# Two chunks of every sequence per block of 512 tokens, units going sequence by sequence, and weight steps set closer together

## The chip, the cores and the metric

The kernel runs on one core of a Trainium2 chip. The metric is device time in microseconds (us): the median of several executions of the same program. A profile is one further execution, recorded by the hardware profiler.

## The reference

Four sequences of 768 tokens go through a retention layer (8 heads of 64) and two feed-forward layers:

```python
for t in range(S):
    state = gamma * state + einsum('bhd,bhe->bhde', k[:, :, t], v[:, :, t])
    y[:, :, t] = scale * einsum('bhd,bhde->bhe', q[:, :, t], state)
x = y.transpose(0, 2, 1, 3).reshape(3072, 512)
h = x @ w_in                                # 512 -> 2048
x = where(h > 0, h, exp(min(h, 0)) - 1) @ w_out
h = x @ w_in2                               # 512 -> 1024
s = h * softmax(h)
out = (s - mean(s)) / sqrt(var(s) + 1e-6) * g_ln @ w_out2
```

All tensors are fp32. `gamma` differs by head and is constant in time.

## The kernel before

**Units and blocks.** The retention is cut into chunks of 64 tokens. A unit is one chunk of one sequence with all 8 heads, 48 units in all, `u = 12 * sequence + chunk`. A block is 512 tokens, so 8 units, and there are 6 blocks; before the change a block is 8 chunks in that order, so a border between sequences can lie inside a block. For a unit TensorE computes the scores (`att_scores`, L191), the product of decayed keys with values that goes into the state (L195), and the values (`att_values`: L232 from the state of the chunk before, which a sequence's first chunk does not have, and L235 from the masked scores). VectorE masks the scores (L199), updates the state (L212; L210 for a first chunk) and writes the scaled output into `xf` (L240). ScalarE copies halves of the state (L215). GpSimd scales the keys (`scale_k`, L185) and makes the decayed state that the next unit adds to (L219). A unit's q, k and v are one load of 576 KB (`load_unit`, L180) into one of four buffers.

**Feed-forward 1.** Each fp32 product is three matmuls of rounded parts: high by high, high by low, low by high (`mm3`, L71 to L73). A slot `s` is one of 16 slices of the hidden width for one block: `ff1_in(s)`, 12 matmuls of 512 columns into `hp`; the ELU (`elu_a` on ScalarE, `elu_b` and `elu_c`); and `ff1_out(s - 2)`, 12 matmuls into `acc`, two slots later.

**Weights.** In block 0 the weights of feed-forward 1 come in as 64-bit words of 512 KB a slice and are turned to fp32 parts on the chip, 32 slices in the order `order1`. The parts of one slice are: `load_w` (SP); `top_w`, a cast on ScalarE and a memset of 16-bit fields on GpSimd (L117, L118); `bits_w`, two shift-and-or operations on VectorE, the second reading the first's result (L124, L125); `high_w`, a cast on ScalarE (L135); `low_w`, a subtraction on VectorE (L143). A call `prep_w(order, n)` issues parts of several slices:

```python
high_w(n - 2); top_w(n + 1); bits_w(n); low_w(n - 2); load_w(n + 3)
```

Two such calls stand in each slot of block 0, and four in the head. Slot `s` of block 0 thereby finishes slices `2s + 1` and `2s + 2`, in the kernel before as in the one after.

**The order.** Every engine runs its instructions in program order, and the program sets that order by hand (`manual_schedule`). The head (L441 to L479) goes through units 0 to 7 of block 0 with no feed-forward work beside them, because the first `ff1_in` needs all 512 tokens. In it units turn through three sets of PSUM banks; two of these later hold `acc`. Where a unit's output is written, `split_x0` makes the high part `xh` (ScalarE, L260) and the low part `xl` (L261; units 0 to 5 on GpSimd, 6 and 7 on VectorE). Then come slots: before the change unit 8 stands in slot 0 and unit `9 + s // 2` in each odd slot, so that block `b`'s units run beside the slots of block `b - 1`. After slot 15 `split_xh` and `split_xl` (L248, L253) cut the next block's tokens. In the last block of feed-forward 1 the second layer's weights are prepared by the same steps in the order `order2`. The rest of the kernel, feed-forward 2 with its normalization by 128 tokens, is not touched except for the rows to which the output goes.

Of the kernel before, what the change touches and what calls it, by code (L numbers as in the profile page):

```python
# [39 lines left out]
PRE = (2, 3, 4, 5)  # L40
AHEAD = 1
# [3 lines left out]
def tile_retention_ffn(ctx, tc, qkv, w_in1, w_out1, w_in2, w_out2, g_ln, dmask, odec, kdec, gdec, ident_in, out):  # L45
# [10 lines left out]
    gm_sb = const.tile([P, 2, 2 * D], F32, name="gm_sb")  # L56
# [5 lines left out]
    kd_sb = small.tile([P, NP], F32, name="kd_sb")  # L62
    g_sb = small.tile([P, NF2], F32, name="g_sb")
    half_n = small.tile([P, 232], F32, name="half_n")[:, :1]
# [10 lines left out]
    with tc.manual_schedule():  # L75
# [8 lines left out]
        e_p = ph1.enter_context(tc.tile_pool(name="e", bufs=3))  # L84
        g_p = ph1.enter_context(tc.tile_pool(name="g", bufs=3))
# [35 lines left out]
        def bits_w(x):  # L121
            raw = raw_t.pop(x)
            low, t = raw[:, :, 0], raw[:, :, 1]
            nc.vector.scalar_tensor_tensor(low, low, 29, top_t.pop(x), ALU.logical_shift_right, ALU.bitwise_or)  # L124
            nc.vector.scalar_tensor_tensor(t, t, 3, low, ALU.logical_shift_left, ALU.bitwise_or)  # L125
            abs_t[x] = t
# [18 lines left out]

        def prep_w(order, n):

            at = lambda i: order[i] if 0 <= i < len(order) else None
# [29 lines left out]
        def load_unit(u):  # L178
            t = at_p.tile([P, 18 * D], F32, tag="in", name="in", bufs=4)
            nc.sync.dma_start(out=t, in_=qkv[u])  # L180
            in_t[u] = t

        def scale_k(u):
            kt = in_t[u][:, KR:KR + 4 * D].rearrange("p (h d) -> p h d", h=4)
            nc.gpsimd.tensor_tensor(kt, kt, kd_sb.unsqueeze(2).to_broadcast([P, 4, D]), ALU.mult)  # L185

        def att_scores(u, banks):
# [4 lines left out]
            if u % NCH < NCH - 1:  # L192
# [9 lines left out]
        def att_state(u, v):  # L202

            c = u % NCH
            if c == NCH - 1:
                return
            st = at_p.tile([P, 2, 2 * D], F32, tag="state", name="state")
# [5 lines left out]
            s2 = at_p.tile([P, 2 * D], F32, tag="s2", name="s2")  # L213
            for j in range(2):
                nc.scalar.copy(s2[half(1 - j)], st[half(j), 1 - j])  # L215
            s_t[u + 1] = (st, s2)
            if c + 1 < NCH - 1:
                sg_t[u + 1] = at_p.tile([P, 2, 2 * D], F32, tag="sg", name="sg", bufs=1)
                nc.gpsimd.tensor_tensor(sg_t[u + 1], st, gm_sb, ALU.mult)  # L219

        def att_values(u, banks):
            c = u % NCH
# [14 lines left out]
        def att_done(u, v):  # L237
            ci = u % UPB
# [17 lines left out]
        def split_x0(ts, engine):  # L256
            if 0 not in x_t:
                x_t[0] = [x_p.tile([P, KD, TB], F32R, tag=tag, name=tag) for tag in ("xh", "xl")]
            xh, xl = x_t[0]
            nc.scalar.copy(xh[:, :, ts], xf[:, :, ts])  # L260
            engine.tensor_tensor(xl[:, :, ts], xf[:, :, ts], xh.bitcast(F32)[:, :, ts], ALU.subtract)  # L261
# [3 lines left out]
        def ff1_in(s):  # L265
# [4 lines left out]
            for cc in range(KD):  # L270
                o = cc * P
                mm3(hp, wh[:, o:o + P], wl[:, o:o + P], xh[:, cc, :], xl[:, cc, :], cc == 0, cc == KD - 1)
# [54 lines left out]
        N2 = NT // P  # L327
        yin, ysp, h2, zc_t, rs_t, zt_t, op_t, zr_t = {}, {}, {}, {}, {}, {}, {}, {}
# [97 lines left out]
        def ff2_out(i, kks=range(NF2)):  # L426
# [26 lines left out]
        scale_k(1)  # L453
        att_scores(0, sets[0][0])
        att_mask(0, sets[0][1])
        att_state(0, sets[0][1])
        load_unit(2)
        slot = -1
        for u in range(UPB):
# [7 lines left out]
            if u < 2:  # L467
                load_w(order1[u])
# [184 lines left out]
```

## Time and profile before

| | |
|---|---|
| median of 3 runs | 892.26 us (891.64 to 892.56) |
| the profiled execution | 892.1 us, span 890.3 us |
| TensorE (PE) busy | 861.9 us, 97% of the span |
| VectorE (DVE) busy | 437.4 us, 49% |
| ScalarE (ACT) busy | 327.1 us, 37% |
| GpSimd (POOL) busy | 336.4 us, 38% |
| moved by DMA | 97.94 MB, mean 110 GB/s |

Busy TensorE time counts matmuls that overlap and whose ends are modelled, so 97% does not say that the array works at its peak. PEclk is the granted clock of TensorE: 1.00 is 2.4 GHz, 0.50 is 1.2 GHz. In a timeline row the text in brackets is the idle time of that engine just before the instruction, and what ended it; "x16" means that 16 instructions of one kind are merged. The first start of an instruction that follows without a pause can lie before the recorded end of the one ahead of it, since they overlap; distances from start to start are what an instruction costs its engine.

### The profile page before, as it was taken

Reading aid. Unit: us, or ns where it says so; the run is one execution under the profiler, and the core shown is the slowest. Engines: PE = TensorE matmul, PEld = TensorE weight load, DVE = VectorE, ACT = ScalarE, POOL = GpSimd, SP = SyncE. Lnnn points to the kernel's source line nnn. Section 1 sums busy time; section 2 is a strip of 40 time slices with the busy share of each in tenths; the row PEclk is TensorE's granted clock in tenths of the full one; section 3 lists DMA queues with packets and bytes.
Section 4 is the critical chain, followed back from the end, with each engine's and each line's share of the span. In section 5 each row is a group of like instructions: output and inputs, shape, how many; then the busy total and the mean of one; then the engine's idle time right before and its main releaser. Section 6 shows DMA issues by size and latency. Waiting matters only on the chain.

```text
span 890.3 us, 15643 instructions
## 1 busy us (share of the span) xinstructions
PE 861.9 (97%) x6432; PEld 703.6 (79%) x6432; DVE 437.4 (49%) x733; ACT 327.1 (37%) x574; POOL 336.4 (38%) x323
## 2 busy tenths in 40 slices
PE   5599999999999999999999999999999999999998
PEld 4478887888888888888888878888778888888886
DVE  3489996222432234222422246786755555555542
ACT  3367774221332232222322234443343333333333
POOL 5545552322333323233323235563333333333330
PEclk9589999999999999999999999999999999999999
DMA  9457762211131112111130024230454444444432
GB/s 322 159 161 229 221 219 72 84 49 33 54 102 54 54 52 78 54 54 54 34 111 16 1 95 154 95 94 25 145 175 142 142 142 145 150 151 147 142 118 72
DMA packets 59879, 97.94 MB, mean 110 GB/s; under 512 B 4896, under 2 KB 41504, under 8 KB 59808
## 3 DMA queue, kind: packets, MB, share of 16 engines
q1 hardware_dynamic: 59808, 96.95, 33.6%
q8 instruction: 50, 0.82, 0.4%
q14 instruction: 21, 0.17, 0.1%
HBM read 72.29 MB, written 24.64 MB: 109 GB/s over the span
## 4 chain that ended last, share of the span: by engine, by line
PE 80%; DVE 12%; DMA 3%; issue 2%; POOL 1%; ACT 1%; SPq 0%; DVEq 0%; ACTq 0%; POOLq 0%
PE hp L72 13%; PE hp L73 13%; PE hp L71 12%; PE acc L71 9%; PE acc L73 8%; PE acc L72 8%; PE op L73 4%; PE op L72 4%; PE op L71 4%; DVE raw L124 2%; DVE raw L125 2%; PE ab L191 1%; DVE w1il L143 1%; DMA in<-in_qkv 1%; DVE w1ol L143 1%
## 5 line engine op out<-in xcount | busy, mean ns | idle before, releaser
L300 POOL TENSOR_TENSOR gl<-e,gh 128x512 fp32r<-128x512 f32 x80 | 108.3, 1354 | 219.2 <-issue 147.8
L71 PE MATMUL hp<-xh,w1ih 128*128 128x512 f32 x384 | 151.9, 396 | 5.1 <-ACT w1ih L135 2.6
L71 PE MATMUL acc<-gh,w1oh 128*128 128x512 f32 x384 | 153.7, 400 | 0.0
L72 PE MATMUL hp<-xl,w1ih 128*128 128x512 f32 x384 | 151.7, 395 | 0.9 <-DVE xl L253 0.9
L73 PE MATMUL hp<-xh,w1il 128*128 128x512 f32 x384 | 151.4, 394 | 0.2 <-DVE w1il L143 0.2
L73 PE MATMUL acc<-gh,w1ol 128*128 128x512 f32 x384 | 150.0, 391 | 0.0
L72 PE MATMUL acc<-gl,w1oh 128*128 128x512 f32 x384 | 149.8, 390 | 0.0
L281 ACT ACTIVATE e<-hp 128x512 f32<-128x512 f32 x80 | 47.7, 597 | 198.6 <-PE hp L73 197.2
L290 DVE TENSOR_SCALAR e<-e 128x512 f32<-128x512 f32 x80 | 36.0, 450 | 147.2 <-ACT e L281 147.2
L292 ACT CAST gh<-e 128x512 fp32r<-128x512 f32 x96 | 59.6, 621 | 97.0 <-DVE e L291 78.1
L71 PEld LDWEIGHTS hp<-xh,w1ih 128*128 128x128 f32 x384 | 73.1, 190 | 20.9 <-ACT xh L260 2.7
L199 DVE TENSOR_TENSOR pt<-ab,dm_sb 128x256 f32<-128x256 f32 x43 | 18.2, 422 | 143.3 <-PE ab L235 133.9
L72 PEld LDWEIGHTS hp<-xl,w1ih 128*128 128x128 f32 x384 | 73.2, 191 | 17.4 <-DVE xl L253 1.6
L73 PEld LDWEIGHTS hp<-xh,w1il 128*128 128x128 f32 x384 | 73.2, 191 | 16.1 <-DVE w1il L143 0.9
L71 PEld LDWEIGHTS acc<-gh,w1oh 128*128 128x128 f32 x384 | 72.1, 188 | 16.2
L73 PEld LDWEIGHTS acc<-gh,w1ol 128*128 128x128 f32 x384 | 72.1, 188 | 16.0 <-DVE w1ol L143 0.5
L72 PEld LDWEIGHTS acc<-gl,w1oh 128*128 128x128 f32 x384 | 72.1, 188 | 14.1
L370 POOL TENSOR_SCALAR z<-z,st 128x1024 f32<-128x1024 f32 x22 | 28.0, 1275 | 140.2 <-DVE st L368 140.2
L73 PE MATMUL op<-w2oh,zl 128*128 128x512 f32 (+1 forms) x192 | 74.2, 386 | 2.6 <-DVE zl L411 2.6
L118 POOL MEMSET raw<- 128x512 uint16 x48 | 60.9, 1269 | 38.4 <-ACT top L117 14.6
L219 POOL TENSOR_TENSOR sg<-state,gm_sb 128x256 f32<-128x256 f32 x40 | 36.1, 902 | 103.0 <-DVE state L212 95.0
L71 PE MATMUL op<-w2oh,zh 128*128 128x512 f32 (+1 forms) x192 | 74.3, 387 | 0.4 <-ACT zh L405 0.4
(112 smaller groups left out, 1450.1 us busy)
## 6 DMA issues: line engine op xcount, KB each, us to landing
in<-in_qkv SPq DMA_DIRECT2D x48, 576.0 KB, 4.4
raw<-in_w_in SPq DMA_DIRECT2D x24, 512.0 KB, 3.6
raw<-in_w_out SPq DMA_DIRECT2D x24, 512.0 KB, 3.6
t_dr<-t SPq DMA_DIRECT2D x22, 512.0 KB, 2.8
zt<-t_dr SPq DMA_DIRECT2D x88, 128.0 KB, 2.5
y_dr<-yt SPq DMA_DIRECT2D x24, 256.0 KB, 2.6
yin<-y_dr SPq DMA_DIRECT2D x24, 256.0 KB, 3.5
out<-ot SPq DMA_DIRECT2D x23, 256.0 KB, 2.7
```

What stands on the lines that cost most here:

```text
L71: nc.tensor.matmul(o, lh, rh, start=first, stop=False)
L72: nc.tensor.matmul(o, lh, rl, start=False, stop=False)
L73: nc.tensor.matmul(o, ll, rh, start=False, stop=last)
L118: nc.gpsimd.memset(quarter(x, 3, U16), 0)
L124: nc.vector.scalar_tensor_tensor(low, low, 29, top_t.pop(x), ALU.logical_shift_right, ALU.bitwise_or)
L199: nc.vector.tensor_tensor(pt, v[:, :, :2 * C], dm_sb, ALU.mult)
L219: nc.gpsimd.tensor_tensor(sg_t[u + 1], st, gm_sb, ALU.mult)
L281: nc.scalar.activation(e, h_t[s], AF.Exp)
L290: nc.vector.tensor_scalar(e, e, 1.0, -1.0, ALU.min, ALU.add)
L292: nc.scalar.copy(gh, e)
L300: engine.tensor_tensor(gl, e, gh.bitcast(F32), ALU.subtract)
L370: nc.gpsimd.tensor_scalar(z, z, st[:, 5:6], 1.0, ALU.add, ALU.mult)
```

## The change

**Order of units.** The input is cut so that block `b` holds chunks `2b` and `2b + 1` of each of the four sequences. Unit `u` has chunk `chunk(u)`; units `u` and `u + 4` are two chunks in a row of one sequence, so the first four units have no state, and four states are kept. `place(u)` puts the four sequences' 128 tokens side by side in `xf`; the output rows of 128 tokens are mapped back by `row(i)`.

**The head** is written anew. Per unit `u` the order is: loads from a table, `scale_k(u + 1)`, `att_decay(u + 1)` (the decayed state, now made when the later unit is near, by a broadcast table that is loaded together with the key decays), `att_state(u)`, `att_scores(u + 1)`, `att_mask(u + 1)`, `att_values(u)`, `att_kv(u + 1)` (the L195 product, now apart from the scores), then weight parts and splits from the tables `MID` and `END`. All `xl` parts go to VectorE. Units 0 to 3 and 7 load into a pool of four buffers that is closed after the head, all other units into three buffers; before there were four for all.

**Slot 0** does its products with `xh` first and the four with `xl` last. Unit 8 is processed in slot 1 (its scores still in the head), unit `8 + s // 2` in each odd slot up to 13, unit 15 in slot 14, unit 16 in slot 15 and from there as before.

**Weight steps.** `bits_w` is cut in two: `bits_w` (first operation) and `merge_w` (second). A step finishes a slice in one go.

```diff
+        def merge_w(x):
+            low, t = abs_t[x]
             nc.vector.scalar_tensor_tensor(t, t, 3, low, ALU.logical_shift_left, ALU.bitwise_or)
             abs_t[x] = t
...
         def prep_w(order, n):
-            if at(n - 2):
-                high_w(at(n - 2))
-            if at(n + 1):
-                top_w(at(n + 1))
-            if at(n):
-                bits_w(at(n))
-            if at(n - 2):
-                low_w(at(n - 2))
-            if at(n + 3):
-                load_w(at(n + 3))
+            step_w(merge_w, order, n)
+            step_w(high_w, order, n)
+            step_w(bits_w, order, n + 1)
+            step_w(low_w, order, n)
+            step_w(top_w, order, n + 2)
+            step_w(load_w, order, n + 4)
...
         def load_unit(u):
-            t = at_p.tile([P, 18 * D], F32, tag="in", name="in", bufs=4)
+            pool, n = (first_p, 4) if u < 4 or u == UPB - 1 else (at_p, 3)
+            t = pool.tile([P, 18 * D], F32, tag="in", name="in", bufs=n)
...
+        chunk = lambda u: u // UPB * (UPB // B) + u % UPB // B
+        place = lambda u: u % B * (UPB // B) + u % UPB // B
...
-            s_t[u + 1] = (st, s2)
-            if c + 1 < NCH - 1:
-                sg_t[u + 1] = at_p.tile([P, 2, 2 * D], F32, tag="sg", name="sg", bufs=1)
-                nc.gpsimd.tensor_tensor(sg_t[u + 1], st, gm_sb, ALU.mult)
+            s_t[u + B] = (st, s2)
+
+        def att_decay(u):
+            if 0 < chunk(u) < NCH - 1:
+                sg_t[u] = at_p.tile([P, 2, 2 * D], F32, tag="sg", name="sg", bufs=SG)
+                four = lambda t: t.rearrange("p a (m d) -> p (a m) d", m=2)
+                nc.gpsimd.tensor_tensor(four(sg_t[u]), four(s_t[u][0]), kg_sb[:, 1].unsqueeze(2).to_broadcast([P, 4, D]), ALU.mult)
...
+            if s == 0:
+                terms = [(w, xh, cc) for cc in range(KD) for w in (wh, wl)] + [(wh, xl, cc) for cc in range(KD)]
+                for i, (w, x, cc) in enumerate(terms):
+                    nc.tensor.matmul(hp, cut(w, cc), x[:, cc, :], start=i == 0, stop=i == len(terms) - 1)
...
+        LOADS = {0: (2, 3, "0"), 1: (4,), 2: (5,), 3: (6,), 4: (7, "1"), 5: (8,), 6: ("2", "3", 9), 7: ("4", 10)}
+        MID = {4: (w(bits_w, 0),), 5: (w(merge_w, 0),), 6: (xl(0, 1, 2, 3),)}
+        END = {
+            3: (w(top_w, 0), xh(0, 1, 2, 3)),
+            5: (w(high_w, 0), xh(4, 5)),
+            6: (xh(6),),
+            7: (xh(7), w(low_w, 0), w(top_w, 1), xl(4, 5), xl(6), xl(7), w(bits_w, 1), w(top_w, 2), w(merge_w, 1)),
+        }
         nc.gpsimd.memset(half_n, -0.5)
         new_top()
+        nc.sync.dma_start(out=kg_sb, in_=kgdec)
         load_unit(0)
         nc.sync.dma_start(out=dm_sb, in_=dmask)
-        nc.sync.dma_start(out=kd_sb, in_=kdec)
         load_unit(1)
-        nc.sync.dma_start(out=gm_sb, in_=gdec)
         nc.sync.dma_start(out=od_sb, in_=odec)
...
         for u in range(UPB):
...
+            banks, v = sets[u % 3]
+            nxt, w = sets[(u + 1) % 3] if u + 1 < UPB else both
+            for x in LOADS.get(u, ()):
+                load_unit(x) if isinstance(x, int) else step_w(load_w, order1, int(x))
+            scale_k(u + 1)
+            if u + 1 >= B:
+                att_decay(u + 1)
+            att_state(u, v)
+            att_scores(u + 1, nxt)
+            att_mask(u + 1, w)
+            att_values(u, banks)
+            att_kv(u + 1, nxt)
+            for f in MID.get(u, ()):
+                f()
+            att_done(u, v)
+            for f in END.get(u, ()):
+                f()
+        first.close()
...
+        att_state(UPB, both[1])
+        scale_k(UPB + 1)
+        att_decay(UPB + 1)
+        step_w(high_w, order1, 1)
+        step_w(bits_w, order1, 2)
+        step_w(low_w, order1, 1)
+        slot = 1
...
-            u = UPB + AHEAD + s // 2 if s % 2 else (UPB if s == 0 else NU)
+            u = UPB + s // 2 + (s > NF1 - 2) if s % 2 else (2 * UPB - 1 if s == NF1 - 2 else NU)
...
                     att_scores(u + 1, both[0])
+                    att_kv(u + 1, both[0])
...
+                if u + 2 < NU:
+                    att_decay(u + 2)
...
-                load_w(order2[0])
-                load_w(order2[1])
-                prep_w(order2, -1)
+                for i in range(-4, 0):
+                    prep_w(order2, i)
```

`step_w(f, order, i)` calls `f` for slice `i` unless that was done already. In `LOADS` a number is a unit and a string a weight slice.

## Rows read from the trace of the kernel before

**Rows 1.** The page's chain of waits that ended last, shares of the span

```profile
PE 80%; DVE 12%; DMA 3%; issue 2%; POOL 1%; ACT 1%; SPq 0%; DVEq 0%; ACTq 0%; POOLq 0%
```

**Rows 2.** Windows: busy us (x instructions) of PE, PEld, DVE, ACT, POOL; PEclk, DMA share, GB/s

```profile
20.00:25.00 5.00, 2.44 (x75) 1.81 (x70) 3.69 (x5) 2.11 (x5) 5.00 (x5) 0.50 0.99 399
...
36.10:41.90 5.80, 5.76 (x16) 3.83 (x17) 0.74 (x1) 0.00 (x0) 1.34 (x2) 0.52 0.29 119
...
100.00:110.00 10.00, 10.00 (x57) 7.98 (x59) 9.69 (x17) 7.24 (x14) 6.41 (x6) 1.00 0.69 236
```

**Rows 3.** Timeline, TensorE, head: start us, us, what [idle before <- releaser]

```profile
18.41 0.71 PE L191 MATMUL acc<-in 64*64 64x64 f32 x16 [0.92 <-DMA in<-in_qkv]
...
21.03 0.70 PE L191 MATMUL ab<-in 64*64 64x64 f32 x15
...
31.61 0.49 PE L232 MATMUL acc<-in,state 64*64 64x64 f32 x8 [2.81 <-DVE state L212]
...
36.14 0.80 PE L71 MATMUL hp<-xh,w1ih 128*128 128x512 f32 x1 [2.55 <-ACT xh L260]
```

**Rows 4.** Timeline, GpSimd and VectorE, head

```profile
20.48 2.35 POOL L261 TENSOR_TENSOR xl<-xf,xh 128x1024 fp32r<-128x1024 f32 x1
...
21.72 1.65 DVE L124 SCALAR_TENSOR_TENSOR raw<-raw,top 128x512 uint32<-128x512 uint32 x1
...
36.12 0.74 DVE L261 TENSOR_TENSOR xl<-xf,xh 128x512 fp32r<-128x512 f32 x1 [1.38 <-ACT xh L260]
```

**Rows 5.** DMA over 0 to 30 us: GB/s in 40 slices; unit loads, us to landing

```profile
GB/s 0 0 117 264 392 240 203 296 350 283 425 410 418 425 434 383 402 296 245 300 414 329 264 390 381 401 417 385 408 404 436 412 410 154 61 18 0 0 0 0
...
in<-in_qkv SPq DMA_DIRECT2D x9, 576.0 KB, 5.9
```

**Rows 6.** Timeline, VectorE, block 0: slot 1's unit, one pair of slots, the split

```profile
52.93 0.42 DVE L199 TENSOR_TENSOR pt<-ab,dm_sb 128x256 f32<-128x256 f32 x1 [2.81 <-PE ab L235]
...
88.37 0.42 DVE L199 TENSOR_TENSOR pt<-ab,dm_sb 128x256 f32<-128x256 f32 x1
...
89.36 0.69 DVE L124 SCALAR_TENSOR_TENSOR raw<-raw,top 128x512 uint32<-128x512 uint32 x1
...
90.15 1.04 DVE L125 SCALAR_TENSOR_TENSOR raw<-raw 128x512 uint32<-128x512 uint32 x1
...
91.12 1.10 DVE L143 TENSOR_TENSOR w1ol<-raw,w1oh 128x512 fp32r<-128x512 f32 x1
...
92.14 0.68 DVE L288 SCALAR_TENSOR_TENSOR e<-e,hp 128x512 f32<-128x512 f32 x1
...
92.74 0.68 DVE L124 SCALAR_TENSOR_TENSOR raw<-raw,top 128x512 uint32<-128x512 uint32 x1
...
93.52 0.69 DVE L125 SCALAR_TENSOR_TENSOR raw<-raw 128x512 uint32<-128x512 uint32 x1
...
100.62 0.42 DVE L199 TENSOR_TENSOR pt<-ab,dm_sb 128x256 f32<-128x256 f32 x1
...
138.50 1.89 DVE L253 TENSOR_TENSOR xl<-xf,xh 128x512 fp32r<-128x512 f32 x3
```

**Rows 7.** Timeline, ScalarE, slot 0 and slot 1

```profile
42.58 0.63 ACT L279 ACTIVATE e<-e 128x512 f32<-128x512 f32 x1
...
48.07 0.69 ACT L135 CAST w1ih<-raw 128x512 fp32r<-128x512 f32 x1
...
48.66 0.77 ACT L117 CAST top<-raw 128x512 f16<-128x512 bf16 x1
```

**Rows 8.** Timeline, TensorE, block 0: two units and what follows them

```profile
85.58 0.46 PE L191 MATMUL ab<-in 64*64 64x64 f32 x16
...
86.44 0.50 PE L71 MATMUL acc<-gh,w1oh 128*128 128x512 f32 x1
...
97.55 0.46 PE L191 MATMUL ab<-in 64*64 64x64 f32 x16
...
98.64 0.50 PE L71 MATMUL acc<-gh,w1oh 128*128 128x512 f32 x1
```

More of the change, by code (lines that the diff above doesn't have):

```diff
@@ L59, in tile_retention_ffn @@
     xf = const.tile([P, KD, TB], F32, name="xf")
-    kd_sb = small.tile([P, NP], F32, name="kd_sb")
+    kg_sb = small.tile([P, 2, NP], F32, name="kg_sb")
     g_sb = small.tile([P, NF2], F32, name="g_sb")
-    half_n = small.tile([P, 232], F32, name="half_n")[:, :1]
+    half_n = small.tile([P, HALF_N], F32, name="half_n")[:, :1]
     t_dr = [dram.tile([4, 4, 32, 2 * P], F32, name=f"t_dr{i}") for i in range(3)]
@@ L83, in tile_retention_ffn @@
         x_p = ph1.enter_context(tc.tile_pool(name="x", bufs=1))
-        e_p = ph1.enter_context(tc.tile_pool(name="e", bufs=3))
-        g_p = ph1.enter_context(tc.tile_pool(name="g", bufs=3))
+        first = ExitStack()
+        first_p = first.enter_context(tc.tile_pool(name="first", bufs=4))
         right = ExitStack()
@@ L144, in low_w, with step_w @@
             dsts[name][f] = (hi, lo)
[L146 to L158 removed]
+        done = set()
+        def step_w(f, order, i):
+            if 0 <= i < len(order) and (f, order[i]) not in done:
+                done.add((f, order[i]))
+                f(order[i])
+        def prep_w(order, n):
+            step_w(merge_w, order, n)
[4 more added lines that the diff above has]
+            step_w(load_w, order, n + 4)
         order1 = [("w1i", 0), ("w1i", 1), ("w1i", 2)]
@@ L202, in att_state @@
         def att_state(u, v):
-            c = u % NCH
+            c = chunk(u)
             if c == NCH - 1:
                 return
-            st = at_p.tile([P, 2, 2 * D], F32, tag="state", name="state")
+            st = at_p.tile([P, 2, 2 * D], F32, tag="state", name="state", bufs=B + 1)
             kv = v[:, :, 4 * C:4 * C + 2 * D]
@@ L237, in att_done @@
         def att_done(u, v):
-            ci = u % UPB
+            ci = place(u)
             four = lambda t: t.rearrange("p (a o) t -> p a o t", a=2)
@@ L253, in split_xl, with split_x0 @@
                 nc.vector.tensor_tensor(xl[:, cc], xf[:, cc], xh.bitcast(F32)[:, cc], ALU.subtract)
-        def split_x0(ts, engine):
+        def split_x0(us, high):
             if 0 not in x_t:
                 x_t[0] = [x_p.tile([P, KD, TB], F32R, tag=tag, name=tag) for tag in ("xh", "xl")]
-            xh, xl = x_t[0]
-            nc.scalar.copy(xh[:, :, ts], xf[:, :, ts])
-            engine.tensor_tensor(xl[:, :, ts], xf[:, :, ts], xh.bitcast(F32)[:, :, ts], ALU.subtract)
+            a, n, step = place(us[0]), len(us), place(us[-1]) - place(us[0])
+            cut = lambda t: t.rearrange("p k (u t) -> p k u t", t=C)[:, :, a:a + step + 1:step // max(n - 1, 1) or 1]
+            xh, xl = (cut(t) for t in x_t[0])
+            if high:
+                nc.scalar.copy(xh, cut(xf))
+            else:
+                nc.vector.tensor_tensor(xl, cut(xf), xh.bitcast(F32), ALU.subtract)
         h_t, g_t, acc_t = {}, {}, {}
@@ L327, in tile_retention_ffn @@
         N2 = NT // P
+        row = lambda i: i % B * S + i // B * P
         yin, ysp, h2, zc_t, rs_t, zt_t, op_t, zr_t = {}, {}, {}, {}, {}, {}, {}, {}
@@ L621, in _layouts @@
     kdec = ga[..., None] ** (C - 1.0 - t)
[L622 removed]
+    gdec = gj ** C
     return {
```

65 lines of the change are left out of this document (24 added, 41 removed).

## The prediction

> **What bounds the kernel now.** I read the page first, for the chain of waits, then windows over the start, then the timeline. The chain that sets the end lies on TensorE for 80% and on VectorE for 12% [rows 1]. The windows and the timeline show three stages. **The head**, to 36.14 us, runs attention units 0 to 7; TensorE waits in it, and its first FFN matmul starts at 36.14 [rows 3]. **Block 0**, to about 139 us: in 100 to 110 us VectorE is busy for 9.69 of 10 us, TensorE by the records for all 10 [rows 2]. One pair of slots takes VectorE 12.25 us without a pause (88.37 to 100.62, [rows 6]), TensorE 11.97 to about 12.2 (85.58 to 97.55, [rows 8]). The two are level, and I take VectorE as the one that is late. **Everything after** belongs to TensorE, and the change can only shift it. So the question is when VectorE reaches the split of block 1's tokens, which starts at 138.50 [rows 6].
>
> The profiled execution took 892.1 us (span 890.3), the median is 892.26; the sum is made against 892.1. About 0.2%, 1.8 us, can be told from no change.
>
> **The head.** Today each unit needs the state of the unit before: at 31.61 TensorE has waited 2.81 us for it [rows 3], an update on VectorE. GpSimd's `xl` takes 2.35 us, and L124 beside it 1.65 us [rows 4]. Units 5 and 6 start 2.6 us apart (18.41, 21.03), the first after a wait for its load [rows 3]: since unit 4 each unit's load goes with one weight load, and each waits for one of four buffers.
>
> After the change the first four units have no state before them, the next four use states that are four units old, and units 0 to 6 have seven buffers, so their loads need no wait. I follow the loads. Unit 1 keeps its place in SP's queue, fourth, and lands after 5.9 us of flight [rows 5], at 8.0. Behind it come `od_sb` (0.13 MB), units 2 and 3, one weight, units 4 and 5 (0.59 MB each, the weight 0.52): at 410 GB/s, the level of the full slices [rows 5], unit 5 lands at 8.0 + 3.01/0.41 = 15.4. Unit 8 needs unit 4's buffer, read by unit 4's values: these follow unit 5's scores, and three overlapping groups of 16 small matmuls, 0.71 us each alone [rows 3], take some 1.6 us, so SP can ask at 17.0. Unit 8 is what comes last: from below it lands at 21.0 (units 6, 7, one weight and itself back to back, 2.29/0.41 = 5.6 us after 15.4), from above at 17.0 + 5.9 = 22.9, with the flight that head loads have now [rows 5]. I take 22.0, the middle. Two weights and unit 9 stand behind it in SP's queue; the first is wanted about 3 us after it could land.
>
> Behind unit 8 stand its scores and unit 7's values, again three groups, taken in full at 2.1 us; unit 7's output on VectorE, 0.4 (as L199, [rows 6]); its cast on ScalarE, 0.4 (0.69 at twice the size, [rows 7]); 0.1 of hand-over. **T0, the first FFN matmul, comes at 25.0 instead of 36.14**, from 23.5 (the early landing, groups overlapping) to 28.5 (the late one, and two weight steps of 2 us ahead of a unit's output).
>
> What moved on to VectorE: the low part of units 0 to 5. By 0.74 us for 512 elements [rows 4] it is some 1.3 for units 0 to 3, under unit 8's flight, and 1.5 for units 4 to 7, of which only the last 0.4 was there before. These run after T0 beside slot 0's matmuls; the new order puts the four products with `xl` last, eight matmuls later, so TensorE does not see them. Taking T0 as given, I charge nothing; without that cover it is 1.5 us. The 3 decays fewer on GpSimd, the smaller decay table and the two tables in one load are nothing as well: GpSimd has room once `xl` is gone. Stated cost if not: 0.5 us.
>
> The loads of block 0, the output rows (again 128 in sequence) and the second FFN's weights, ready two steps earlier, keep a slot or more of room: nothing.
>
> **From T0 to VectorE's chain.** Slot 0's 12 matmuls took at most 5.7 us at clock 0.52 [rows 2]. Then Exp 0.63 [rows 7] and ahead of it Relu, of the same shape, the ELU on VectorE 0.6, one weight step 2.0, `gl` 0.6: VectorE reaches slot 1's unit at T0 + 10.2 = 35.2. Today that is at 52.93, after idle stretches, the last of 2.81 us [rows 6], because unit 8 stands in slot 0 and the second weight comes late. Gain 17.7 us.
>
> The clock was at half (1.2 GHz) in the head and slot 0 [rows 2], and TensorE had sat idle for 2.55 us ahead of slot 0 [rows 3]. The Trainium skill ("TensorE: Matmul & The Clock Gate", Part 1) says that the clock rises after sustained activity and falls after idling. By it a denser head could leave slot 0 at full clock: 2.8 instead of 5.7 us, and a total about 2.7 us lower; I keep the row's half clock.
>
> **The rest of block 0** took VectorE 138.50 - 52.93 = 85.6 us. It changes by:
> - one more unit, since unit 8 moves from slot 0 to slot 1: three instructions in 1.0 (88.37 to 89.36), and two that run beside GpSimd's work and last 1.04 and 1.10, where L125 takes 0.69 at 93.52 [rows 6]: +1.8;
> - weights are 1.5 steps less advanced at this point (two merges and one L124 at 0.60): +1.8;
> - L125 follows directly on L124, which it reads: 0.78 from start to start, where others are 0.60 apart [rows 6]. The new order puts other work between: 29 steps x 0.18 = -5.2;
> - in its place the low part waits for a cast whose input the same step has just merged: merge 0.69, cast 0.69 [rows 7], while VectorE has 1.2 us of other work: 0.2 per step, +5.8. From below 0 (ScalarE's start overlaps), from above 1.0 (below).
>
> Net +4.2, so the split starts at 35.2 + 89.8 = 125.0 instead of 138.5: -13.5. TensorE's own floor lies lower: slot 2 at T0 + 10, then 14 slots x 24 matmuls x 0.231 (11.1 us for 48, [rows 8]) and seven units of 1.09: T0 + 95.2 = 120.2.
>
> **After block 0** units 12, 24 and 36 now have a state before them: 1.09 instead of 0.86 [rows 8], +0.7. Sum: 892.1 - 13.5 + 0.7 = **879.3**.
>
> The load rate is read from slices of 380 to 436 GB/s [rows 5]. The Trainium skill ("DMA: Bandwidth & Descriptors", "Where 436 GB/s comes from") puts loads from HBM at about 358. By that unit 8 lands at 22.9, and the sum would be 880.2; the slices speak against it.
>
> **Rivals.**
> - *TensorE alone ends block 0*: the casts arrive in time. Split at the floor, 120.2: -18.3 + 0.7 = 874.5. For it: the dependency goes. Against: merge plus cast is longer than the work between. 0.17.
> - *Loads still pace the head*: units 2.6 us apart as now; unit 8 comes two such paces after unit 6's 21.03 [rows 3], at 26.2; T0 is 29.2: 883.5. For it: SP still waits for a buffer at units 7 to 10. Against: seven need none. 0.15.
> - *ScalarE's queue takes the place of the gap, slower.* A step's cast stands behind the last step's top cast, Relu and Exp (0.77, then twice 0.63, [rows 7]), and the low part waits for it in the same step, where today it had a step and a half of lead. Less VectorE's work meanwhile, the wait is 1.0 per step: 29 x 0.8 more, 902.5. It decides from 0.64 us a step. Against: ScalarE is busy 7.24 of 10 us [rows 2]. 0.06.
> - *It doesn't do what it says*: the head is held by its amount of work and T0 stays near 35, what is won goes into the weight waits: 892. For it: GpSimd is busy 5.00 of 5 us from 20 to 25 [rows 2]. Against: 2.35 of that is the `xl` that moves away, and VectorE stands at 3.69. 0.04.
>
> My own case has 0.58. The range takes in T0 from 23.5 to 28.5, the step's wait from 0 to 0.4, and most of the first two rivals: 872.5 to 886. Faster 0.88, same 0.04, slower 0.08.
>
> **What would show it.** In the changed profile: the first L71-type matmul of `hp` near 25; no wait of TensorE for a state in the head; its last wait there for the load of unit 8; VectorE in block 0 with steps of about 2.0 us, whose short waits name the cast; the `xl` split of block 1 near 125; later pairs unchanged. T0 past 30 makes the head's step wrong; a split later than T0 + 102, the step in block 0.

## The result, and the profile after

The changed kernel takes **877.22 us** (median of 4 runs, 876.53 to 878.18), the kernel before 892.34 (4 runs): ratio 0.9833, 95% interval 0.9816 to 0.985. The forecast was 879.3, with a range of 872.5 to 886. The profiled execution took 877.41, its span is 875.6 (before: 890.3).

How far the changed kernel is ahead, at marks that both timelines have:

| first instruction of | before | after | lead |
|---|---|---|---|
| T0, slot 0's matmuls | 36.14 | 27.66 | 8.48 |
| slot 2's matmuls | 52.79 | 36.06 | 16.73 |
| `xl` split of block 1 | 138.50 | 124.95 | 13.55 |
| first row maximum of feed-forward 2 | 620.15 | 606.75 | 13.40 |
| second row maximum | 632.86 | 617.63 | 15.23 |
| end of the span | 890.3 | 875.6 | 14.7 |

The page's chain of waits, shares of the span (compare [rows 1]):

```profile
PE 82%; DVE 8%; DMA 4%; ACT 3%; issue 2%; SPq 0%; POOL 0%; DVEq 0%; ACTq 0%
```

VectorE's share fell from 12 to 8%. The timeline of TensorE at the end of the head and in slot 0 (compare [rows 3]):

```profile
23.57 0.71 PE L199 MATMUL ab<-in 64*64 64x64 f32 x16 [0.65 <-DVE xf L254]
...
27.25 0.48 PE L206 MATMUL ab<-in 64*64 64x64 f32 x6 [1.68 <-issue]
27.66 0.79 PE L292 MATMUL hp<-xh,w1ih 128*128 128x512 f32 x1
...
29.11 0.63 PE L292 MATMUL hp<-xh,w1il 128*128 128x512 f32 x1
29.54 0.63 PE L292 MATMUL hp<-xh,w1ih 128*128 128x512 f32 x1
...
32.16 0.39 PE L70 MATMUL hp<-xh,w1ih 128*128 128x512 f32 x1
32.39 0.39 PE L71 MATMUL hp<-xl,w1ih 128*128 128x512 f32 x1
```

The wait of 2.81 us for a state is gone (the longest one left is 0.24), and so is the 2.55 ahead of T0. In their place stand 0.65 for VectorE, which was still busy with low parts, and 1.68 with no releaser ("issue": the engine waited for nothing that the profile shows). From start to start the matmuls of slot 0 are 0.43 us apart, later 0.23: half clock (1.2 GHz) at first, full clock (2.4) from 31.2 on, after TensorE had been busy without a pause since 27.25. The three engines that feed it:

```profile
21.58 1.60 DVE L279 TENSOR_TENSOR xl<-xf,xh 128x1024 fp32r<-128x1024 f32 x1
...
22.05 1.59 POOL L233 TENSOR_TENSOR sg<-state,kg_sb 128x256 f32<-128x256 f32 x1
...
23.10 0.41 DVE L254 TENSOR_TENSOR xf<-ab,od_sb 128x256 f32<-128x256 f32 x1
...
25.65 0.41 ACT L277 CAST xh<-xf 128x256 fp32r<-128x256 f32 x1 [1.07 <-DVE xf L254]
```

The last cast that T0 needs ends at 26.06, 1.6 us ahead of T0.

As much of the lead, 8.25 us, arises between T0 and slot 2. The kernel before, the start of slot 1 on TensorE and the window over that slot (columns as in [rows 2]):

```profile
45.58 0.80 PE L71 MATMUL hp<-xh,w1ih 128*128 128x512 f32 x1 [2.58 <-ACT w1ih L135]
...
45.60:51.50 5.90, 5.74 (x12) 3.62 (x12) 4.42 (x7) 2.50 (x4) 3.62 (x4) 0.50 0.43 113
```

The changed kernel, where slot 1 starts at 32.16, the unit behind slot 1:

```profile
34.97 0.46 PE L199 MATMUL ab<-in 64*64 64x64 f32 x16
```

Before, unit 8 and a wait of 2.58 us for the second weight stand between slots 0 and 1 (41.84 to 45.58), and the 12 matmuls of slot 1 take 5.95 us at half clock. Now slot 1 follows at once and takes 2.81 us at full clock, and slot 0 takes 4.50 instead of 5.70. These differences (3.74, 3.14 and 1.20) and 0.17 from the unit behind slot 1 make up the 8.25. They are read from two traces; no run takes the wait and the clock apart.

Block 0 on VectorE (compare [rows 6]):

```profile
108.03 0.42 DVE L210 TENSOR_TENSOR pt<-ab,dm_sb 128x256 f32<-128x256 f32 x1
...
109.02 0.81 DVE L128 SCALAR_TENSOR_TENSOR raw<-raw 128x512 uint32<-128x512 uint32 x1
109.75 1.10 DVE L123 SCALAR_TENSOR_TENSOR raw<-raw,top 128x512 uint32<-128x512 uint32 x1
110.77 0.68 DVE L146 TENSOR_TENSOR w1ol<-raw,w1oh 128x512 fp32r<-128x512 f32 x1
...
111.97 0.68 DVE L128 SCALAR_TENSOR_TENSOR raw<-raw 128x512 uint32<-128x512 uint32 x1
112.57 0.68 DVE L123 SCALAR_TENSOR_TENSOR raw<-raw,top 128x512 uint32<-128x512 uint32 x1
113.39 0.69 DVE L146 TENSOR_TENSOR w1il<-raw,w1ih 128x512 fp32r<-128x512 f32 x1
...
121.79 0.68 DVE L128 SCALAR_TENSOR_TENSOR raw<-raw 128x512 uint32<-128x512 uint32 x1
123.19 0.69 DVE L146 TENSOR_TENSOR w1ol<-raw,w1oh 128x512 fp32r<-128x512 f32 x1 [0.71 <-ACT w1oh L138]
124.35 0.69 DVE L311 SCALAR_TENSOR_TENSOR e<-e,hp 128x512 f32<-128x512 f32 x1 [0.47 <-ACT e L302]
124.95 2.49 DVE L267 TENSOR_TENSOR xl<-xf,xh 128x512 fp32r<-128x512 f32 x4
```

L128 is the merge, L123 the first shift, L146 the low part. The first shift no longer stands behind what it reads; the low part starts 0.82 us after the shift ahead of it (112.57 to 113.39) where 0.60 is the pace. TensorE at the border to block 1:

```profile
123.80 0.39 PE L72 MATMUL acc<-gh,w1ol 128*128 128x512 f32 x1
124.88 0.49 PE L70 MATMUL hp<-xh,w1ih 128*128 128x512 f32 x1 [0.69 <-ACT xh L262]
125.69 0.50 PE L71 MATMUL hp<-xl,w1ih 128*128 128x512 f32 x1 [0.32 <-DVE xl L267]
```

From slot 4 to slot 14 TensorE's pairs of slots begin exactly 12.20 us apart (49.51, 61.71, ... 98.31, 110.51) and no wait is recorded from 41 to 124 us; VectorE's pairs are 11.81 to 11.88 apart (11.83 from 96.20 to 108.03), also with hardly a pause. So inside block 0 TensorE waits for nobody, and VectorE is late only at the border, by 0.69 and 0.32. (In the kernel before TensorE has no wait from 47.5 to 139 us either.) The 0.69 names a cast on ScalarE. ScalarE had stood 2.58 us for the merge of the last weight slice, and the cast for block 1 stands behind it:

```profile
122.50 0.65 ACT L138 CAST w1oh<-raw 128x512 fp32r<-128x512 f32 x1 [2.58 <-DVE raw L128]
```

Last, the border between the two feed-forward layers on VectorE, first the kernel before (TENSOR_REDUCE takes the row maximum, L320 copies the accumulators of feed-forward 1, L132 and L143 prepare weights of the second layer):

```profile
620.15 1.23 DVE L363 TENSOR_REDUCE st<-hp 128x1 f32<-128x1024 f32 x1 [3.02 <-PE hp L73]
...
627.24 0.48 DVE L132 TENSOR_SCALAR raw<-raw,g_sb 128x512 f32<-128x512 f32 x1
628.43 1.51 DVE L143 TENSOR_TENSOR w2ol<-raw,w2oh 128x512 fp32r<-128x512 f32 x1 [0.72 <-ACT w2oh L135]
629.86 1.28 DVE L320 COPY yt<-acc 128x512 f32<-128x512 f32 x2
...
632.86 1.22 DVE L363 TENSOR_REDUCE st<-hp 128x1 f32<-128x1024 f32 x1
```

Then the changed kernel:

```profile
606.75 1.23 DVE L387 TENSOR_REDUCE st<-hp 128x1 f32<-128x1024 f32 x1 [3.49 <-PE hp L72]
...
614.02 1.29 DVE L343 COPY yt<-acc 128x512 f32<-128x512 f32 x2
617.63 1.23 DVE L387 TENSOR_REDUCE st<-hp 128x1 f32<-128x1024 f32 x1 [2.32 <-PE hp L72]
```

Two maxima are 12.71 apart before and 10.88 after: the last weight slices are done two steps earlier and no longer stand between VectorE and the copies.

### The profile page after: what moved, and what is told of

Same layout as the page of the kernel before. It is cut to its first block, busy times and chain, and to the rows that moved or that the text cites. A ratio compares the mean times of both kernels' runs of the same rounds, so it can differ in the third digit from the quotient of the medians.

```text
span 875.6 us, 15632 instructions
## 1 busy us (share of the span) xinstructions
PE 858.5 (98%) x6432; PEld 703.0 (80%) x6432; DVE 438.3 (50%) x736; ACT 330.6 (38%) x575; POOL 323.0 (37%) x321
## 3 DMA queue, kind: packets, MB, share of 16 engines
HBM read 72.16 MB, written 24.64 MB: 111 GB/s over the span
## 4 chain that ended last, share of the span: by engine, by line
PE 82%; DVE 8%; DMA 4%; ACT 3%; issue 2%; SPq 0%; POOL 0%; DVEq 0%; ACTq 0%
PE hp L71 13%; PE hp L72 13%; PE hp L70 12%; PE acc L70 9%; PE acc L71 8%; PE acc L72 8%; PE op L72 4%; PE op L71 4%; PE op L70 4%; DMA in<-in_qkv 2%; PE ab L199 1%; DVE raw L128 1%; DVE e L311 1%; DVE raw L123 1%; ACT w1ih L138 1%
## 5 line engine op out<-in xcount | busy, mean ns | idle before, releaser
L71 PE MATMUL hp<-xl,w1ih 128*128 128x512 f32 x380 | 148.1, 390 | 0.8 <-DVE xl L267 0.8
L70 PE MATMUL hp<-xh,w1ih 128*128 128x512 f32 x380 | 148.1, 390 | 0.7 <-ACT xh L262 0.7
L72 PE MATMUL hp<-xh,w1il 128*128 128x512 f32 x380 | 147.8, 389 | 0.0
L313 DVE TENSOR_SCALAR e<-e 128x512 f32<-128x512 f32 x80 | 38.5, 481 | 137.3 <-ACT e L304 137.1
L71 PEld LDWEIGHTS hp<-xl,w1ih 128*128 128x128 f32 x380 | 71.3, 188 | 16.2 <-DVE xl L267 1.5
L70 PEld LDWEIGHTS hp<-xh,w1ih 128*128 128x128 f32 x380 | 71.3, 188 | 16.0 <-ACT xh L262 1.1
L72 PEld LDWEIGHTS hp<-xh,w1il 128*128 128x128 f32 x380 | 71.3, 188 | 14.7
L70 PE MATMUL hp<-w2ih,yh 128*128 128x512 f32 x192 | 74.7, 389 | 0.0
```

Of the source, the lines that this page charges most:

```text
L70: nc.tensor.matmul(o, lh, rh, start=first, stop=False)
L71: nc.tensor.matmul(o, lh, rl, start=False, stop=False)
L72: nc.tensor.matmul(o, ll, rh, start=False, stop=last)
L313: nc.vector.tensor_scalar(e, e, 1.0, -1.0, ALU.min, ALU.add)
```

## The experiments

Totals below are to be read against the kernel before on the same chip (891.06 to 891.72 us on four chips). The changed kernel was repeated on one of them, beside the runs with the old steps in block 0 and those with empty queues; for the runs on other chips the ratios are compared (0.9833 above, 0.9849 repeated).

**The changed kernel again.** 

> The changed kernel itself, as the measure for the three runs beside it: ratio to the kernel before 0.981 to 0.985, first FFN matmul (T0) at 27.2 to 27.8 after TensorE's gap at its 961st instruction, the split of block 1 near 125.

877.48 us (877.1 to 879.2), ratio 0.9849 (0.9834 to 0.9864). T0 is 28.69 in this profile, later than expected, the wait with no releaser ahead of it is 2.77 us, and the split of block 1 starts at 126.81. This profiled execution took 879.2, the other three 877.1 to 877.56. So T0 of one kernel differs by 1.0 us between two profiles, and smaller differences of T0 below say little by themselves.

### The steps of the second layer's weights

```diff
-                for i in range(-4, 0):
+                for i in range(-4, -2):
...
-                prep_w(order2, k)
+                prep_w(order2, k - 2)
...
-                prep_w(order2, NF1 + k)
+                prep_w(order2, NF1 + k - 2)
```

> The changed kernel with the second layer's weight steps two steps later, as they stood before. My theory, from the trace after: the lead over the kernel before grows from 13.4 to 15.2 us between the first and the second row maximum of feed-forward 2, because VectorE's queue no longer holds two weight slices there. It expects that growth to go: 1.5 to 1.8 us slower than the changed kernel, about 878.8 us. Rival (the prediction): these steps have room in either place, within 0.4 us of the changed kernel's 877.2.

880.41 us (879.68 to 882.82), ratio 0.9879 (0.986 to 0.9897): by the ratios 2.7 to 4.1 us slower than the changed kernel, more than the theory said. The interval just touches that of the repeated kernel. The split of block 1 stays at 124.95; the two row maxima are 14.25 apart instead of 10.88. The new steps made late cost 3.4 us there, more than the old steps did (12.71).

The other way round, the kernel before with its old steps for the second layer two earlier:

```diff
-                load_w(order2[0])
-                load_w(order2[1])
-                prep_w(order2, -1)
+                for i in range(2):
+                    load_w(order2[i])
+                for i in (-1, 0, 1):
+                    prep_w(order2, i)
...
-                prep_w(order2, k)
+                prep_w(order2, k + 2)
...
-                prep_w(order2, NF1 + k)
+                prep_w(order2, NF1 + k + 2)
```

> The kernel before with only the second layer's weight steps two steps earlier. Theory: 1.5 to 1.8 us faster than before, about 890.6 us, ratio 0.998, with no late copies of the accumulators on VectorE at the border of the layers. Rival (the prediction): no change, 892.1 to 892.5.

889.32 us against 891.06, ratio 0.9983 (0.997 to 0.9996); the maxima are 10.89 apart. In the kernel before this part alone is worth 1.7 us (0.4 to 2.7 by the interval). The effect is shown both ways, though not with one size, and I had put it at nothing.

### The steps of block 0

```diff
+        def prep_old(order, n):
+            step_w(high_w, order, n - 2)
+            step_w(top_w, order, n + 1)
+            step_w(bits_w, order, n)
+            step_w(merge_w, order, n)
+            step_w(low_w, order, n - 2)
+            step_w(load_w, order, n + 3)
...
-                prep_w(order1, slot)
+                prep_old(order1, slot)
```

> The changed kernel with block 0's weight steps in the old order (cast and subtraction two slices behind the shift operations). Theory: a step costs VectorE 2.00 us in the old order and 2.03 in the new one, and TensorE sets the pace of block 0 (pairs of 12.20 against VectorE's 11.87), so the split moves by less than 1.2 us and the total by less than 1.2 us, slower if at all. Rival (the closer steps carry a large part of the gain): 3 us or more slower.

877.59 us (876.06 to 878.47), ratio 0.9845 (0.9829 to 0.9861): no difference in the total. TensorE's pairs are 12.20 apart here too, with both of VectorE's shifts one behind the other again. At the border the old steps are better:

```profile
124.46 0.39 PE L70 MATMUL hp<-xh,w1ih 128*128 128x512 f32 x1
124.68 0.39 PE L71 MATMUL hp<-xl,w1ih 128*128 128x512 f32 x1
```

No wait, since the low parts start at T0 + 96.66 instead of T0 + 97.29. So closer steps bring block 0 nothing, and cost 1.0 us at its end. The total does not show the 1.0: in the profiled execution (878.47) the split comes 1.54 us earlier than in the changed kernel, 0.91 of it from an earlier T0 (26.75), and the first row maximum 1.19 earlier (605.56). The rest of the way takes it back, as told below for the empty queues; here too the granted clock is 0.50 for 3.4 us, from about 636.5 on.

### What T0 waits for

The low parts of units 0 to 3 behind the end of the head:

```diff
-        MID = {4: (w(bits_w, 0),), 5: (w(merge_w, 0),), 6: (xl(0, 1, 2, 3),)}
+        MID = {4: (w(bits_w, 0),), 5: (w(merge_w, 0),)}
...
-            7: (xh(7), w(low_w, 0), w(top_w, 1), xl(4, 5), ...
+            7: (xh(7), w(low_w, 0), w(top_w, 1), xl(0, 1, 2, 3), xl(4, 5), ...
```

> The changed kernel with the low part of units 0 to 3 moved from ahead of unit 6's output to after T0. Theory, from the trace after: unit 8's scores waited for that output (0.65 us) and not for unit 8's load; the scores start 0.65 us earlier, at about 22.9, T0 comes 0.6 earlier, and the total falls by 0.5, to 876.7. Rival (the prediction: unit 8's load comes last): T0 and total unchanged.

877.38 us, ratio 0.9846 (0.9826 to 0.9866). Unit 8's scores come earlier (its mask at 22.88 instead of 24.34), but T0 stays at 27.66: TensorE now waits 3.38 us, again with no releaser, at the same instruction. That instruction is the first after 961 recorded ones on TensorE, in each of these runs, and shorter waits of the kind stand after 450 and 706. The trace's queue of instruction transfers (50 of 16 KB, for 12,864 matmuls and weight loads) shows one that starts at 24.91 us in the changed kernel, 25.99 when repeated, 24.95 here; TensorE goes on at 27.25, 28.27, 27.25, always 2.3 us later. The next runs try to show that it starts late because the DMA queues are full. First fewer weights in flight, by four buffers instead of five and a later load of unit 9:

```diff
-        LOADS = {..., 6: ("2", "3", 9), 7: ("4", 10)}
+        LOADS = {..., 6: ("2",), 7: ("3", "4", 9, 10)}
...
-        stage_p = ph0.enter_context(tc.tile_pool(name="stage", bufs=5, side="right"))
+        stage_p = ph0.enter_context(tc.tile_pool(name="stage", bufs=4, side="right"))
```

> The changed kernel with four weight buffers and unit 9 loaded after three weights, so that from 25 us few bytes are under way. Theory A: TensorE's 1.68 us gap in the middle of a group ahead of T0 is its instruction fetch (16 KB, 24.9 to 25.8) held up by the full DMA queues: the gap falls under 1 us, T0 to about 26.9, total 876.5. Theory B: the fetch is late by itself, whatever the load: gap, T0 and total as in the changed kernel, within 0.3 us.

878.57 us (874.71 to 881.67), ratio 0.9851 (0.9828 to 0.9874). The transfer starts at 24.37, the wait is 1.90, T0 27.21: inconclusive, as the loads still fill the queues until then. Next, nothing at all behind unit 8 until the first weight's low part is out (the third weight takes the first one's buffer, and its steps come one later):

```diff
-        LOADS = {..., 6: ("2", "3", 9), 7: ("4", 10)}
+        LOADS = {..., 6: ()}
...
-            7: (xh(7), w(low_w, 0), w(top_w, 1), ...
+            7: (xh(7), w(low_w, 0), w(load_w, 2), lambda: load_unit(9), w(load_w, 3), w(load_w, 4), lambda: load_unit(10), w(top_w, 1), ...
```

> The changed kernel with the third weight loaded into the first one's buffer, and units 9 and 10 and two more weights asked for behind it, so that between about 21 and 26 us only unit 8 is under way. Theory (the gap ahead of T0 is TensorE's fetch of its next 256 instructions, which stands in the full DMA queues from its 706th instruction at 20.3 to 24.9): the fetch moves by 23, the gap at the 961st instruction goes, T0 comes at about 26.1, where the last cast ends, and block 0 ends 1.0 to 1.5 us earlier. Rival (the fetch has a pace of its own): the gap stays over 1 us and T0 within 0.3 us of the changed kernel's.

And the same with the low parts of units 0 to 3 behind the end of the head, as above:

> The same, with the low part of units 0 to 3 after T0 as well. Fetch theory: with the fetch out of the way the 0.65 us that unit 8's scores waited for VectorE now counts: T0 at 25.4 to 25.6, total 1.5 to 2 us under the changed kernel. Rival: no change in T0, as when that part alone was moved.

878.56 us (ratio 0.9861, 0.9844 to 0.9877) and 877.39 (0.9847, 0.9832 to 0.9861). The windows from 21.5 to 25 us (PE, PEld, DVE, ACT, POOL busy; PEclk, DMA share, GB/s), the changed kernel first, then the second of these runs (the changed kernel's trace has no record of the clock before 31.2, so its 1.00 here says nothing):

```profile
21.50:25.00 3.50, 2.85 (x100) 2.66 (x104) 2.76 (x5) 1.48 (x5) 2.15 (x2) 1.00 1.01 342
```

```profile
21.50:25.00 3.50, 2.89 (x100) 2.51 (x91) 2.14 (x5) 1.62 (x6) 1.18 (x2) 0.50 0.02 5
```

With the queues empty the instruction transfer starts at 21.56 and 21.21, and the wait is gone in both. T0 is 25.94 in the first run, but TensorE then waits 1.50 us for the second weight, and block 0 ends no earlier (split at 125.08), against the theory. The second run:

```profile
25.05 0.79 PE L292 MATMUL hp<-xh,w1ih 128*128 128x512 f32 x1 [0.56 <-ACT xh L277]
...
30.71 0.50 PE L70 MATMUL hp<-xh,w1ih 128*128 128x512 f32 x1 [1.13 <-ACT w1ih L138]
```

T0 is 25.05, the value of the forecast, 2.6 us earlier. The total does not follow. The second weight is late (1.13), as its cast stands behind a state copy; slot 2 is 1.0 us earlier than in the changed kernel (35.08), and the first row maximum still is (605.69). Then feed-forward 2's first product with `zh`, which needs a chain of transfers through DRAM, starts at 634.21 against 634.69: half of the 1.0 is gone. The rest of what the profiled execution lost (it took 878.19, the other three 877.36 to 877.42) lies in the matmuls that follow: the granted clock is 0.50 from 635.9 to 639.3, where the changed kernel has 1.00, and nine matmuls take 3.65 us (635.80 to 639.45) instead of 2.07 (636.28 to 638.35). The lead of 0.48 us turns into a lag of 1.1. Ahead of it TensorE had waited 1.21 and 0.52 us; in the changed kernel, which kept the full clock, 0.64 and 0.53.

### What held the head before

The wait of 2.81 us for a state in [rows 3] ended with an update that stood in VectorE's queue. The kernel before, VectorE, while TensorE was waiting:

```profile
28.85 1.71 DVE L143 TENSOR_TENSOR w1il<-raw,w1ih 128x512 fp32r<-128x512 f32 x1
...
31.15 0.41 DVE L212 TENSOR_TENSOR state<-sg,acc 128x256 f32<-128x256 f32 x1
```

Three operations on weights (L124, L125, L143, from 26.80 to 30.56), a mask and an output were ahead of it. The changed kernel has fewer weight operations in its head; no run puts them back.

In the first of three runs every unit of the head adds to the state of the unit just before it, as before the change:

```diff
-            s_t[u + B] = (st, s2)
+            if u + 1 < UPB:
+                s_t[u + 1] = (st, s2)
+            if u >= UPB - B:
+                s_t[u + B] = (st, s2)
...
-            if u + 1 >= B:
-                att_decay(u + 1)
             att_state(u, v)
+            att_decay(u + 1)
```

> The changed kernel, but in the head every unit again adds to the state of the unit just before it (units 1 to 7 thus use states of other sequences, and three of them values and decays that they did not have); from unit 8 on as changed. Marks: the last cast of the high part starts at 25.65 in the changed kernel, T0 at 27.66. Theory (the dependency by itself is cheap in the head: an update of 0.41 us on VectorE and a decay of 0.61 on GpSimd make 1.2 us with the hand-overs, less than the 1.4 to 2.7 us between two landings of units): last cast by 27.2, T0 27.7 to 29.2, total within 1.6 us of 877.4. Rival (the dependency is what kept the units 2.6 us apart before): last cast past 30, T0 past 31, total over 880.5.

876.42 us (2 runs), ratio 0.9833 (0.9811 to 0.9856). The last cast of the high part moves by 1.46 to 27.11, T0 not at all (27.57). Of the 1.46, 1.08 are the instruction wait: units with a state have more matmuls, so the 961st record falls into unit 8's scores (25.80), ahead of unit 7's values, where the changed kernel has it behind them. The dependency by itself costs about 0.4 us at the last cast and nothing that T0 shows. Then the same with the low parts of units 0 to 5 back on GpSimd:

```diff
-                nc.vector.tensor_tensor(xl, cut(xf), xh.bitcast(F32), ALU.subtract)
+                (nc.gpsimd if us[0] < 6 else nc.vector).tensor_tensor(xl, cut(xf), xh.bitcast(F32), ALU.subtract)
...
-            3: (w(top_w, 0), xh(0, 1, 2, 3)),
-            5: (w(high_w, 0), xh(4, 5)),
+            3: (w(top_w, 0), xh(0, 1, 2, 3), xl(0, 1, 2, 3)),
+            5: (w(high_w, 0), xh(4, 5), xl(4, 5)),
```

> The chained head of the run before, and in addition the low parts of units 0 to 5 back on GpSimd, right behind their high parts as in the kernel before. Theory (what held the head before was GpSimd: its 2.35 us for four low parts stand in front of a decay for which the next unit waits): TensorE waits again for a state, 1 to 3 us in one place near 18 to 24; last cast 1 to 3.5 us later than with the chain alone, T0 29 to 32, total 1 to 3.5 us above the chain alone. Rival (the work of the head or its loads pace it either way): last cast within 0.6 us of the chain alone.

879.33 us (2 runs), ratio 0.9866 (0.9847 to 0.9885): 2.9 us more, and T0 30.62, 3.05 later. The timelines of TensorE and GpSimd:

```profile
18.66 2.54 POOL L283 TENSOR_TENSOR xl<-xf,xh 128x1024 fp32r<-128x1024 f32 x1 [2.43 <-ACT xh L281]
21.17 0.60 POOL L190 TENSOR_TENSOR in<-in,kg_sb 128x256 f32<-128x256 f32 x1
...
21.83 0.71 PE L207 MATMUL acc<-in 64*64 64x64 f32 x16 [2.59 <-POOL in L190]
...
25.68 1.26 POOL L283 TENSOR_TENSOR xl<-xf,xh 128x512 fp32r<-128x512 f32 x1 [1.90 <-ACT xh L281]
26.90 0.61 POOL L190 TENSOR_TENSOR in<-in,kg_sb 128x256 f32<-128x256 f32 x1
...
27.57 0.46 PE L207 MATMUL acc<-in 64*64 64x64 f32 x16 [1.52 <-POOL in L190]
```

TensorE waits for scaled keys (L190), not for a state: they stand behind the low parts in GpSimd's queue. The theory had the size right and the waiting operation wrong. Both runs have instruction waits as well, 1.15 and 1.08 us with the chain alone and 2.28 here (at 15.71), about the same in sum, so the 3 us are GpSimd's.

Third, four buffers for the unit loads of the head instead of seven:

```diff
-            pool, n = (first_p, 4) if u < 4 or u == UPB - 1 else (at_p, 3)
+            pool, n = (first_p, 4) if u < UPB else (at_p, 3)
```

> The changed kernel with four buffers for the loads of all eight units of block 0, as before the change, in place of seven; nothing else. Units 4 to 7 then ask for their load only when the values of the unit four before are done (near 8.6, 10.5, 12.5 and 14.4 us by the rows of the changed kernel, where today they ask at 4.7 to 8.7). Theory (the transfers are the limit at this pace, not the room: unit 4 lands at 13.07 however early it asks, and 0.59 MB take 1.4 us): units 4 to 7 land within 1.2 us of 13.07, 15.61, 16.99 and 18.36, the last cast of the high part within 0.8 us of 25.65, T0 within 0.8 us of 27.66, total within 1.6 us of 877.4. Rival (the room is what frees the head, as the prediction had it): unit 7 lands past 20, the last cast past 27.5, T0 past 29, total over 878.5.

878.64 us (2 runs), ratio 0.9855 (0.9827 to 0.9884). Neither theory: unit 7 lands at 21.65 instead of 18.36, as the rival says, but the last cast comes only 0.33 later (25.98) and T0 no later (27.47). The 1.2 us more in the total (ratio 0.9855 against 0.9849) are no more than two runs on another chip can leave open. T0 hides this as it hides the chain, since the instruction transfer (24.64) sets it.

### A version from these findings

```diff
-HL = NF1 - 2
+HL = NF1 - 1
...
-        LOADS = {..., 6: ("2", "3", 9), 7: ("4", 10)}
+        LOADS = {..., 6: ("2",)}
-        MID = {4: (w(bits_w, 0),), 5: (w(merge_w, 0),), 6: (xl(0, 1, 2, 3),)}
+        MID = {4: (w(bits_w, 0),), 5: (w(merge_w, 0),)}
...
-            6: (xh(6),),
-            7: (xh(7), w(low_w, 0), w(top_w, 1), xl(4, 5), xl(6), xl(7), w(bits_w, 1), w(top_w, 2), w(merge_w, 1)),
+            6: (xh(6), w(top_w, 1)),
+            7: (xh(7), w(low_w, 0), lambda: load_unit(9), w(load_w, 3), w(load_w, 4), lambda: load_unit(10), w(bits_w, 1), xl(0, 1, 2, 3), w(merge_w, 1), w(high_w, 1), w(top_w, 2), xl(4, 5), xl(6), xl(7)),
...
+            if i == 1:
+                turn(i)
+                turned(i)
             if i + 2 < N2:
                 split_y(i + 2)
-            if i < N2 - 1:
+            if 1 < i < N2 - 1:
```

> The changed kernel with four edits. Of the loads behind unit 8 only one weight goes out before the head's last output, the others behind the low part of the first weight; the second weight is prepared ahead of the low parts of the tokens; the last slice of feed-forward 1's weights is finished behind the split of block 1's tokens; in the first row of feed-forward 2's loop the transposition goes ahead of the split that waits for a load. Theory (the fetch of TensorE's next instructions waits behind the queued loads; TensorE, not VectorE, sets block 0 until its border, where VectorE is late): the wait at TensorE's 961st instruction under 0.8 us, T0 25.0 to 26.2, the third slot's first matmul at 34 to 35 (36.06 in the changed kernel), no wait over 0.5 us at the border of blocks 0 and 1, where the low parts start near 120.5 to 122 (124.95); total 873.5 to 875.5. Rival (the border of the two feed-forward layers takes back what is won, as it did when T0 alone came earlier): 876.5 to 878.

875.88 us (873.43 to 876.86, 5 runs), ratio 0.9824 (0.9806 to 0.9841), against 0.9833 and 0.9849 for the changed kernel. The intervals overlap, so it is not shown to be faster, and the total is above the range that the theory gave. Its marks came as it said: T0 26.13, slot 2 at 34.53, low parts at 120.85, no wait at the border. The first edit did not do what it was for: SP asks for unit 9 at 19.83 and for two more weights at 20.20 and 20.67, as buffers for them are free, and the instruction transfer starts at 23.44. TensorE does not show it, because it has a new wait ahead of T0:

```profile
23.37 1.25 POOL L117 MEMSET raw<- 128x512 uint16 x1 [2.90 <-ACT top L116]
24.43 1.00 POOL L190 TENSOR_TENSOR in<-in,kg_sb 128x256 f32<-128x256 f32 x1
...
25.49 0.71 PE L206 MATMUL ab<-in 64*64 64x64 f32 x16 [2.22 <-POOL in L190]
```

The second weight's memset, which I had moved forward, now stands in GpSimd's queue ahead of unit 8's keys.

## Why the prediction was right, and where its steps were wrong

The total was right, by a mechanism that was half right and by errors that cancel. At the split of block 1 the errors are +2.66 (T0), -0.94 (T0 to slot 1's unit) and -1.77 us (the rest of block 0). That they leave 124.95 where 125.0 was said is luck.

- **The head** was said to end at T0 = 25.0; it ended at 27.66. Unit 8's landing was well placed (21.35, from bounds of 21.0 to 22.9), and the forecast's rate from the slices of [rows 5] holds: 408 GB/s on average from 3.75 to 17.25 us, in slices of 357 to 436. But the load is not what comes last, and 0.65 us of VectorE's low parts, which I had put under unit 8's flight at nothing, are: 1.60 us for four, beside a decay on GpSimd (1.59). The larger part, 1.68, is the instruction transfer, in no row that I had read for what it is: the profile of before has a wait of 0.89 with "issue" at 22.62.
- **Why the head was long before** I got half right. I named the dependency on the unit before, GpSimd's `xl` and the buffers. The 2.81 us that I gave to the dependency were VectorE's queue of weight operations. The runs show GpSimd's queue, 3 us of T0's 8.5; the dependency alone and the buffers alone show nothing at T0. The other 5.4 are not taken apart by a run. In the kernel before GpSimd also had three more weights' memsets there, 1.25 us each, and weight loads between the units' (unit 7 landed at 24.68, now at 18.36). That these and VectorE's weight operations are the rest is argued only.
- **From T0 to slot 1's unit** took VectorE 9.26 us, not 10.2 (36.92). The 12 matmuls of slot 0 took 4.5 us instead of 5.7, because the clock rose at 31.2 within the slot, where I had kept the half clock of before. The Trainium skill ("TensorE: Matmul & The Clock Gate", Part 1) says that the clock rises after sustained activity. The trace agrees, but the rise came behind T0 and not ahead of it. (The gain by that rule, 2.8 for 5.7, is 2.9 us by its own terms, not 2.7.)
- **Rest of block 0**: 88.03 us on VectorE, not 89.8. The dependency's 0.18 and the cast's 0.2 per step were sized right (0.82 instead of 0.60 is seen). The added unit was too dear: beside GpSimd the operations lose 0.34 us per unit (0.73 and 1.02 from start to start where 0.60 and 0.81 stand alone), in [rows 6] 0.78. Most of the units that were there before save the difference too, which the sum did not have, nor the two waits of VectorE at the border (0.71 and 0.47).
- **Who sets block 0** was the wrong step. I took VectorE to be late by 4.8 us, over a floor of TensorE at 120.2. The floor is 124.19, the end of slot 15's last matmul, and VectorE is late by 0.76. T0 came 2.66 later than in the floor's sum; slot 2 starts at T0 + 8.4 instead of 10; eight units stand in slots 2 to 15, not seven (unit 16 is in slot 15); and slot 2 takes 6.69 us, where 5.44 is the pace, with waits for its weights at 39.42 and 40.35. The first rival was thus right in its mechanism from slot 2 to the border and wrong in its time. The dependency (-5.2) and the cast (+5.8), on which the sum for VectorE rests, decide nothing: with the old steps the total is no different.
- **After block 0** I charged 0.7 for three units with a state; the lead fell by 0.17 from the first split to the last (by 0.94 up to the fourth split, of which 0.77 came back by the fifth). The second layer's steps, at nothing, gave 1.8. Without them the marks give 892.1 - 13.4 = 878.7, near the forecast.
- **The other rivals.** Loads do not pace the head as they did (TensorE's waits for one are 0.24 and 0.21 us, at 13.12 and 15.65); ScalarE's queue takes 0.22 per step, not the 0.64 from which it decides. A T0 near 35 is excluded by 27.66.

## What to carry to other kernels

When two engines are level over a stage, count the slots and units of both to the last instruction before saying which is late, and look at the border of the stage apart from its inside: here it has another limit. A helper engine with a mixed queue (GpSimd with keys, decays, low parts and memsets) holds the critical engine through whichever of its operations stands behind the long one, in the changed version as well. A gain that is real at one mark has to be followed to the last mark: T0 moved by 2.6 us and the total by nothing, since 1.6 of it was lost by slot 2, mostly to the second weight, which was now the late one, and the rest at the border of the layers and behind it.

## What the hardware showed unexpectedly

TensorE's own instructions arrive by DMA, in transfers of 16 KB, and behind full queues they arrive late: at a DMA share of 1.01 the transfer starts at 24.91 (23.44 to 25.99 in the other runs with full queues), and in eight of these ten runs TensorE stands for 1.08 to 3.38 us ahead of T0; at 0.02 it starts at 21.21 (21.56 in the other such run) and TensorE does not stand. The Trainium skill ("Runtime: NRT & Kernel Launch", "Instruction fetch mechanics") says that instructions come in blocks of 256, which the waits after 450, 706 and 961 instructions agree with, and that crossing a block's end is "mostly hidden", which these waits contradict for a head that loads as fast as it can.
